# Two layers forward and backward on one core: the first MLP's order of work, a second load of K, and rows turned inside a norm's wait

## The chip, the core and the metric

The kernel runs on one core of a Trainium2 chip. The metric is the device time of one execution in microseconds (us); of the kernel before there are three runs, with a median of 460.42 us (459.21 to 463.47). One more execution was profiled, and every line of a profile comes from that one: it took 461.23 us, with a span of 459.2 us from the first to the last instruction. TensorE's granted clock was 0.629 of full speed on average.

## The reference: what is computed

Two identical decode layers, one token, with weights shared by both, and then the gradients of all inputs for a given `grad_out`:

```python
x = A_x
x = x + attn(layernorm(x)); x = x + mlp(layernorm(x))   # layer 0
x = x + attn(layernorm(x)); x = x + mlp(layernorm(x))   # layer 1
# attn: q = x @ wq (32 heads of 128); the last 4096 of 32768 keys and values, 4 groups of heads
#       p = softmax(q k / sqrt(128)); (p v) @ wo
# mlp:  h = x @ w1 + b1; act = h * tanh(softplus(h)); act @ w2
out, vjp = jax.vjp(f, x, k_cache, v_cache, wq, wo, w1, b1, w2)
return out, *vjp(grad_out)
```

All data are bf16. D = 1024, wq is 1024 x 4096, wo 4096 x 1024, w1 1024 x 3584, w2 3584 x 1024. The gradients of the two caches are as large as the caches (2 x 32 MB); all of them but the last 4096 rows of each group is zero.

## The kernel before: how the work is tiled and staged

The token is one column, so a product with a weight matrix is a row of 128 x 128 weight loads with a moving operand of one column (`mv`, L460; the loops at L493, L573, L621 and L673). A gradient product needs the same matrix turned. For that a row block of a tile is either turned on TensorE (`turned`, L446: eight transposes into a PSUM bank of `big()`, a copy back over the tile by VectorE or ScalarE through `evac`, L297, and eight products some rows later through `later`, L434), or it is multiplied with a broadcast vector and summed on VectorE (`rowdot`, L420). `rows_chunk` (L466) takes the four row blocks of a tile of wo or w2: the first `nr` go to `rowdot`, the others to `turned`. There are three banks `BIG` for all of that; SC[1] is lent as a fourth in the wq stages (L902).

The stages, in order of time: norm, q, scores, softmax, p v, wo of layer 0 (to 70 us); h of the first MLP (to 88); the first MLP's w2 products, with the row blocks of w2 turned for the later gradient in between (L719 to L727), to 105; the attention of layer 1 (to 150.5); its MLP's h (to 161); eight turnings of K and V (`conv(8, "A")`, L767); then backward: w1 of layer 1 (`dn_b1`, 170 to 191), wo of layer 1 (192 to 221), scores (to 232), wq (to 260; its result is the gradient g2 that goes into the next stage), w2 with layer 1's forward products beside it (L1097 to L1102, 262 to 288), w1 of layer 0 (`dn_b0`, to 298), wo (to 321), scores and wq of layer 0 (to 352). From there to 437 the outer products of the weight and cache gradients are made and copied out (the tail), and stores go on to the end.

K and V must stand the other way round in the backward pass than in the forward pass. `conv_units` (L591) lists 32 units of eight blocks, 16 of K and 16 of V; `conv` turns some in place wherever it is called: one after the scores (L514), one in the softmax (L530), one after each wo tile of layer 1 (`wo_hook1`, L740), eight after the MLP (L767), two after each wo tile backward (L955) until none is left. `w1_rest` (L780) does the like for eight units of w1, for use in `dn_b0`: two behind the scores' gradient, two behind dq (`dp3`, `dq3`), four within wq (`dn3`).

What sets the order is the program's own order on each engine and two queues of transfers. SP's queue loads the weights: a `Ring` (L38) of eight slots of 1,024 KB. Loads stand in a fixed list (L272 to L288) and go out when a slot is released; a released slot takes the next one on the list. Five tiles of wq are kept from layer 0 to layer 1 (`KEEP_Q`), so in the first MLP three slots turn round. w2's tile 3 has `zt` as its home (L282). POOL's queue writes the zero part of the cache gradients: 56 blocks of 1,024 KB out of `zt`, which must have been cleared (L728) after tile 3 was used. `zeros(n, after)` (L256) issues n of them; `after` is a value for which POOL waits first.

`ln_bwd` (L391) is the norm's gradient: two small sums on VectorE, one product with `onesD` on TensorE (L406), four small operations on VectorE. Its `beside` is called ahead of and behind that product; only the last stage gives one. The product of a norm and its result leave TensorE waiting.

Of the kernel before, what the change touches and what calls it, by code (L numbers as in the profile page):

```python
# [18 lines left out]
D = 1024  # L19
# [74 lines left out]
def kernel(  # L94
# [296 lines left out]
    def ln_bwd(part, n32, rstd, g, name, beside=None):  # L391

        st = tmp([P, 2], FP32, "bst")
        dn = tmp([P, TD], FP32, "dn")
        t2 = tmp([P, TD], FP32, "t2")
        if part is None:
            nc.vector.tensor_scalar(out=dn[:], in0=TP[:, 0:TD], scalar1=1.0, scalar2=0.0, op0=ALU.mult, op1=ALU.add,
                                    accum_out=st[:, 0:1])
        else:
            nc.vector.scalar_tensor_tensor(out=dn[:], in0=TP[:, 0:TD], scalar=1.0, in1=part[:], op0=ALU.mult, op1=ALU.add,  # L400
                                           accum_out=st[:, 0:1])
        nc.vector.scalar_tensor_tensor(out=t2[:], in0=dn[:], scalar=1.0, in1=n32[:], op0=ALU.mult, op1=ALU.mult,
                                       accum_out=st[:, 1:2])
        if beside is not None:
            beside()
        nc.tensor.matmul(TP[:, 128:130], lhsT=onesD[:], rhs=st[:], start=True, stop=True)  # L406
        if beside is not None:
            beside()
        ab = tmp([P, 2], FP32, "ab")
        nc.vector.tensor_copy(ab[:], TP[:, 128:130])  # L410
        nc.vector.scalar_tensor_tensor(out=t2[:], in0=n32[:], scalar=ab[:, 1:2], in1=dn[:], op0=ALU.mult,
                                       op1=ALU.subtract)
        nc.vector.tensor_scalar(out=t2[:], in0=t2[:], scalar1=ab[:, 0:1], scalar2=rstd[:, 0:1], op0=ALU.add,
                                op1=ALU.mult)
        gn = sb([P, TD], FP32, f"g_{name}")
        nc.vector.tensor_sub(gn[:], g[:], t2[:])
        return gn
# [27 lines left out]

    def turned(w, n, mv, eng=None, block=None):  # L446

        b = big().bitcast(BF16)
        for i in range(n):
            nc.tensor.transpose(b[:, i * P:(i + 1) * P], block(w, i) if block else w[:, i * P:(i + 1) * P], ident_bf[:])  # L450
        evac(w, b[:, 0:n * P], eng, cost=(0.69 * n / 8, n / 8))
        later(mv, True)

# [11 lines left out]

    def rows_chunk(ch, c, col, l, vec, dst, off, nr=2, eng="A"):  # L466

        for tt in range(4):
            r = 4 * c + tt
            if tt < nr:  # L470
                rowdot(ch[:, tt, :], [vec], D, dst[:, r:r + 1])
            else:
                w = ch[:, tt, :]
                turned(w, TD, lambda w=w, r=r: mv(w, TD, TP[:, off + r:off + r + 1], lambda i: col[:, i, l:l + 1], True), eng)

# [5 lines left out]
    def attn_fwd(l, x, st, first, wo_hook, q_hook=None):  # L481
# [4 lines left out]
        if q_hook is not None:  # L486
            q_hook()
        q_ps = MV[:, 0:HQ]
        order = list(range(TD)) if l == 0 else sorted(range(TD), key=lambda t: t not in KEEP_Q)
        for k, t in enumerate(order):  # L490
# [4 lines left out]
            if l == 0 and t in KEEP_Q:  # L495
                ring.keep(("q", 0, t), ("q", 1, t))
            else:
                ring.release(("q", l, t))
        qv = QC[:].rearrange("p v (g u l h) -> p v g u l h", g=G, u=2, l=2)
        nc.vector.tensor_scalar(out=qv[:, 0, :, 0, l, :], in0=q_ps.rearrange("p (g h) -> p g h", g=G), scalar1=scale,  # L500
# [12 lines left out]
        if not first:  # L513
            conv(1, "A")  # L514
        nc.vector.tensor_tensor(out=m64[0][:], in0=m64[0][:], in1=m64[1][:], op=ALU.max)
        m32 = small[:, 128:160]
# [12 lines left out]
        if not first:  # L529
            late = conv_pe(1)  # L530
        for i in range(2):
# [18 lines left out]
        for u in range(2):  # L550
            nc.tensor.matmul(TP[:, 256:288], lhsT=onesD[:], rhs=ssv[:, :, u, :], start=(u == 0), stop=(u == 1))

        rs = small[:, 288:320]
        nc.vector.tensor_scalar(out=rs[:], in0=TP[:, 256:288], scalar1=float(D), scalar2=None, op0=ALU.mult)
# [35 lines left out]

    conv_units = [(KT, g, b8) for g in range(G) for b8 in range(4)] + [(VS, g, b8) for g in range(G) for b8 in range(4)]  # L591
    conv_units.reverse()
# [22 lines left out]
    def mlp_fwd(l, x, st):  # L615
        name = f"B{l}"
        n32, rstd = ln_fwd(x, st, NB[:, :, l], name)
        h_ps = MV[:, 192:192 + TF]
        for t in range(TD):
# [98 lines left out]
    mv_open()  # L718
    for c in range(7):  # L719
        ch = ring.get(("2", 0, c))  # L720
        mlp_out(0, ch, c, y_ps)
        flush()
        if c in EARLY_2:
            ring.release(("2", 0, c))
        elif c < 6:
            rows_chunk(ch, c, GB, 1, gbc, da1, DA)
            later(lambda c=c: ring.release(("2", 0, c)))  # L727
    nc.gpsimd.memset(zt[:], 0.0)  # L728
    x2, st2 = residual(y_ps, x1, "B0")


    def last_da():

        rows_chunk(ring.get(("2", 0, 6)), 6, GB, 1, gbc, da1, DA)
        flush()
        ring.release(("2", 0, 6))
        v = da1[:, 8:TF].rearrange("p (a b) -> p a b", b=4)[:, :, 2:4]
        nc.vector.tensor_copy(v, TP[:, DA + 8:DA + TF].rearrange("p (a b) -> p a b", b=4)[:, :, 2:4])

    def wo_hook1(c):  # L740
        if c == 0:
            zeros(7, OC[:, 0, 1:2])
        conv(1)

# [21 lines left out]
    put_by("NB", NB, TD)  # L766
    conv(8, "A")  # L767
    mp1 = sB1["deriv"]()
# [22 lines left out]
    def dn_b1(g):  # L791
# [10 lines left out]
        flush()  # L802
        return ln_bwd(dnp, sB1["n32"], sB1["rstd"], g, "B1")

# [21 lines left out]
    def dn_b0(g):  # L826
        bcast(lambda c: DHC[:, c, 0:1], STAY)
        mv_open()
        for t in range(TD):
# [8 lines left out]
            if t == 4:  # L838
                rowize_f()
        return ln_bwd(dnp, sB0["n32"], sB0["rstd"], g, "B0")  # L840

    DENSE = 2

    def attn_bwd(l, sv, g, wo_key, wq_key, wq_keep, hooks, beside=None):
# [6 lines left out]
        for c in range(8):  # L851
            ch = ring.get((*wo_key, c))

            behind[0] = max(2, 6 - max(0, c - DENSE + 1))
            rows_chunk(ch, c, GA, l, LB[0], do32, DA, 0 if c < DENSE else 1, None)
            later(lambda c=c: ring.release((*wo_key, c)))
            hooks["do"](c)
# [86 lines left out]
    def dq3():  # L944
        w1_rest(2)
        zeros(4, DQC[:, 0, 1:2])

    def dn3(t):
        if t % 2:
            w1_rest(1)  # L950
        if t in (3, 5):
            zeros(1, dnp[:, t:t + 1])

    g2 = attn_bwd(1, sA1, g3, ("o", 1), ("q", 2), KEEP_Q2,
                  dict(do=lambda c: conv(2), dp=dp3, dq=dq3, dn=dn3))  # L955


# [137 lines left out]
    mv_open()  # L1095
    even()
    for c in range(7):  # L1097
        ch = ring.get(("2", 1, c))
        mlp_out(1, ch, c, y_ps)
        flush()  # L1100
        rows_chunk(ch, c, GB, 0, LB[0], da0, DA)
        later(lambda c=c: ring.release(("2", 1, c)))  # L1102
    flush()
    rows_join(da0, TF, DA)
    nc.vector.tensor_tensor(out=dh0[:], in0=da0[:, 0:TF], in1=mp0[:], op=ALU.mult)
    nc.vector.tensor_copy(DHC[:, :, 0], dh0[:])
# [37 lines left out]
    def dn1(t):  # L1144
        if t in (3, 6, 7):
            zeros(2 if t == 3 else 1, dnp[:, t:t + 1])
        if t == 4:
# [3 lines left out]

    def units_a0():

        even()
        load["D"] += 10
        work(4)
# [51 lines left out]
```

## Time and profile before

| what | value |
|---|---|
| median of three runs | 460.42 us (459.21 to 463.47) |
| profiled execution | 461.23 us, span 459.2 us |
| TensorE products busy | 341.7 us, 74% |
| VectorE, ScalarE, POOL busy | 256.6, 225.0, 38.7 us |
| moved by DMA | 179.38 MB, 391 GB/s on average |
| SP's queue, POOL's queue | 119.74 MB, 58.72 MB |
| zero blocks | 56 of 1,024 KB, first issued at 120.9 us, last at 350.1 us |

A line of a timeline has the start in us, the length, engine, line, operation, what is written and what is read, the count, and in brackets how long the engine was idle before and what released it. A line of the windows has the stretch, its length, the busy time of TensorE (products, then weight loads), VectorE, ScalarE and POOL with the number of instructions, the granted clock, the share of the 16 DMA engines and the rate in GB/s.

### The profile page before, as it was taken

The page shows a single profiled execution, that of the slowest core. Times are in us where ns is not written, and L with a number is a line of the kernel's source. Part 1 is how long each engine was busy: PE and PEld are TensorE (multiplying, and loading weights), DVE is VectorE, ACT ScalarE, POOL GpSimd, SP SyncE. Part 2 cuts the span into 40 slices and gives each one's busy share as a digit, 9 for nine tenths or more (in the row PEclk, how much of TensorE's full clock was granted, in tenths as well). Part 3 has the DMA queues.
Part 4 walks back from the last instruction along what each step waited for, and adds up shares of the span by engine and source line. Part 5 has one row for each costly group of instructions (what it writes and reads, how often), then busy time and mean ns, then how long its engine had stood idle before and what let it go on. Part 6 is the DMA issues. An engine that isn't in the chain of part 4 may idle for free. (4 is left out here: it accounts for less than half of the span.)

```text
span 459.2 us, 14200 instructions
## 1 busy us (share of the span) xinstructions
PE 341.7 (74%) x6361; PEld 276.6 (60%) x6361; DVE 256.6 (56%) x516; ACT 225.0 (49%) x261; POOL 38.7 (8%) x85
## 2 busy tenths in 40 slices
PE   3836445598679888598879798798797888889900
PEld 3735434497569887498779798697693222224600
DVE  4505731283060149677528676657456999998810
ACT  2502001055045379377317555157064999999900
POOL 1000000030103322200211000101221000000000
PEclk9955555555555569699759955589586555555555
DMA  8999999877999999999999988999999999999995
GB/s 337 421 420 418 418 419 416 361 278 261 385 425 422 421 417 418 415 399 415 420 422 418 421 320 298 347 344 368 422 419 424 412 422 422 418 421 416 405 407 213
DMA packets 27802, 179.38 MB, mean 391 GB/s; under 512 B 3642, under 2 KB 3670, under 8 KB 9430
## 3 DMA queue, kind: packets, MB, share of 16 engines
q1 hardware_dynamic: 19586, 119.74, 65.5%
q0 software_dynamic: 8064, 58.72, 30.9%
q8 instruction: 49, 0.80, 0.6%
q14 instruction: 11, 0.09, 0.0%
q10 hardware_dynamic: 92, 0.02, 0.0%
HBM read 79.74 MB, written 98.62 MB: 388 GB/s over the span
## 5 line engine op out<-in xcount | busy, mean ns | idle before, releaser
L306 ACT COPY ring<-BIG 128x1024 bf16<-128x1024 bf16 x62 | 60.7, 1014 | 41.5 <-PE BIG L450 36.1
L450 PE MATMUL BIG<-ident_bf,ring 128*128 128x128 bf16 x744 | 67.4, 255 | 1.8 <-ACT W L306 1.1
L450 PEld LDWEIGHTS <-ring 128*128 128x128 bf16 x816 | 61.5, 116 | 2.8 <-issue 2.2
L1015 PE MATMUL wide<-W 2*128 2x512 bf16 x228 | 52.1, 598 | 9.3 <-ACT W L306 2.0
L427 DVE CUSTOM_DVE_ANT_0 junk<-ring,SC 128x1024 bf16<-128x1024 bf16 x34 | 41.3, 1215 | 5.4 <-DMA ring<-in_B_w_dram 3.7
L1015 PEld LDWEIGHTS <-W 2*128 2x128 bf16 x240 | 12.6, 102 | 44.3 <-issue 43.2
L462 PEld LDWEIGHTS <-ring 128*128 128x128 bf16 x912 | 31.6, 98 | 9.3 <-ACT ring L306 6.7
L306 ACT COPY KT<-BIG 128x1024 bf16<-128x1024 bf16 x22 | 21.8, 1016 | 30.3 <-PE BIG L602 28.7
L303 DVE CAST ring<-wide 128x1024 bf16<-128x1024 f32 (+1 forms) x29 | 33.7, 1199 | 3.2 <-PE wide L1015 1.5
L306 ACT COPY W<-BIG 128x1024 bf16<-128x1024 bf16 x28 | 26.7, 1119 | 16.0 <-PE BIG L788 14.9
L306 ACT CAST ring<-wide 128x1024 bf16<-128x1024 f32 (+1 forms) x35 | 32.9, 1018 | 1.3 <-PE wide L1066 0.5
L303 DVE COPY ring<-BIG 128x1024 bf16<-128x1024 bf16 x31 | 21.3, 690 | 19.3 <-PE BIG L450 12.2
L264 POOL DMA_DIRECT2D out_dram<-zt x56 | 29.7, 534 | 22.9 <-DMA out_dram<-zt 22.0
L621 PE MATMUL MV<-NB,W 128*128 128x1 bf16 x448 | 16.2, 172 | 9.3 <-DMA W<-in_B_w_dram 6.5
L493 PE MATMUL MV<-NA,ring 128*128 128x1 bf16 x512 | 14.9, 165 | 11.0 <-DMA ring<-in_A_wq_dram 8.6
L621 PEld LDWEIGHTS <-W 128*128 128x128 bf16 x448 | 15.9, 118 | 9.8 <-DMA W<-in_B_w_dram 7.2
L303 DVE CAST VS<-wide 128x1024 bf16<-128x1024 f32 (+1 forms) x17 | 19.7, 1186 | 3.6 <-PE wide L1015 3.0
L1066 PE MATMUL wide<-W 32*128 32x256 bf16 x128 | 20.9, 402 | 0.9 <-ACT ring L306 0.8
L306 ACT CAST KT<-wide 128x1024 bf16<-128x1024 f32 x20 | 20.4, 1032 | 1.8 <-PE wide L1015 0.9
L493 PEld LDWEIGHTS <-ring 128*128 128x128 bf16 x512 | 14.2, 103 | 11.5 <-DMA ring<-in_A_wq_dram 9.1
L427 DVE CUSTOM_DVE_ANT_0 junk<-ring,DSX 128x1024 bf16<-128x1024 bf16 x16 | 19.6, 1224 | 1.1 <-DMA ring<-in_B_w_dram 0.7
L427 DVE CUSTOM_DVE_ANT_0 junk<-W,SC 128x512 bf16<-128x512 bf16 (+1 forms) x20 | 15.8, 791 | 6.5 <-PE SC L330 5.8
(268 smaller groups left out, 566.9 us busy)
## 6 DMA issues: line engine op xcount, KB each, us to landing
out_dram<-zt POOLq DMA_DIRECT2D x56, 1024.0 KB, 16.2
ring<-in_A_wq_dram SPq DMA_DIRECT2D x22, 1024.0 KB
ring<-in_A_wo_dram SPq DMA_DIRECT2D x14, 1024.0 KB
ring<-in_B_w_dram SPq DMA_DIRECT2D x13, 1024.0 KB
W<-in_A_wo_dram SPq DMA_DIRECT2D x10, 1024.0 KB
W<-in_B_w_dram SPq DMA_DIRECT2D x8, 896.0 KB
out_dram<-ring SPq DMA_DIRECT2D x7, 1024.0 KB
out_dram<-ring SPq DMA_DIRECT2D x13, 512.0 KB
```

Of the source, the lines that this page charges most:

```text
L264: nc.gpsimd.dma_start(dst, zt[:])
L303: nc.vector.tensor_copy(dst, src)
L306: nc.scalar.copy(dst, src)
L427: nc.vector.tensor_tensor_reduce(out=out, in0=a, in1=vec, scale=1.0, scalar=acc if i else 0.0, op0=ALU.mult, op1=ALU.add, accum_out=acc)
L450: nc.tensor.transpose(b[:, i * P:(i + 1) * P], block(w, i) if block else w[:, i * P:(i + 1) * P], ident_bf[:])
L462: nc.tensor.matmul(out, lhsT=w[:, i * P:(i + 1) * P], rhs=rhs_of(i), start=fresh[0], stop=last and i == n - 1, skip_group_check=True)
L493: nc.tensor.matmul(q_ps[:, h:h + 1], lhsT=ch[:, h * P:(h + 1) * P], rhs=NA[:, t, l:l + 1], start=(k == 0 and h == 0), stop=(k == TD - 1), ...
L621: nc.tensor.matmul(h_ps[:, fb:fb + 1], lhsT=f_block(W1[:, t], fb), rhs=NB[:, t, l:l + 1], start=(t == 0 and fb == 0), stop=(t == TD - 1), ...
L1015: nc.tensor.matmul(b[:, 512 * i:512 * i + 512], lhsT=R[at:at + 2, lo:lo + P], rhs=R[at:at + 2, ro + 512 * i:ro + 512 * i + 512], start=Tru ...
L1066: nc.tensor.matmul(b[:, k * 256:(k + 1) * 256], lhsT=RT[32 * g:32 * g + 32, a, tp, :], rhs=YS[32 * g:32 * g + 32, :], start=True, stop=Tru ...
```

## The change

Five things are done at once.

- First MLP: the w2 products of tiles 0 to 6 go ahead, and the turnings of tiles 2 to 6 are spread between and behind them. Tile 2's row blocks are turned ahead of the first product; tile 5's and tile 6's after the norm, inside layer 1's q (`last_da` with k). Three zero blocks are issued when `zt` is clear.
- K: one group of four is still turned; the other three are loaded again from the cache, as they lie there, once layer 1's scores are done. 20 units are left, and they are called at other places.
- `w1_rest`: two units leave the place behind dq and go into the w2 stage.
- `turn_ahead`: in the norm that precedes w2, and in the one that precedes layer 0's wo, three row blocks of the next stage's first tile are turned into the three `BIG` banks; `rows_chunk` finds them there and only copies them out. In the w2 stage all four row blocks of tile 0 are turned, and SC[1] is lent as a bank.
- Three zero blocks fewer in layer 0's wq stage.

```diff
+    def turn_pe(w, n, block=None):
         b = big().bitcast(BF16)
         for i in range(n):
             nc.tensor.transpose(b[:, i * P:(i + 1) * P], ...)
+        return b
+    def turn_ev(w, b, n, eng=None):
         evac(w, b[:, 0:n * P], eng, cost=(0.69 * n / 8, n / 8))
+    ahead = {}
+    def turn_ahead(key, tts):
+        for tt in tts:
+            ahead[key, tt] = turn_pe(ring.get(key)[:, tt, :], TD)
...
+                if (key, tt) in ahead:
+                    turn_ev(w, ahead.pop((key, tt)), TD, eng)
+                    later(f, True)
+                else:
+                    turned(w, TD, f, eng)
...
         if not first:
             conv(1, "A")
+            for g in range(K_TURNED, G):
+                nc.sync.dma_start(KT[:, g], kv_src(A_k_cache, g))
...
-            late = conv_pe(1)
+            late = conv_pe(2)
...
+    K_TURNED = 1
+    conv_units = [(KT, g, b8) for g in range(K_TURNED) ...] + [(VS, g, b8) for g in range(G) ...]
...
+    da_turn(2)
+    for c in range(3):
+        da_out(c)
         if c in EARLY_2:
             ring.release(("2", 0, c))
+    da_put(2)
+    da_dots(2)
+    da_out(3)
+    da_turn(3)
+    da_put(3)
+    da_dots(3)
+    da_mv(2)
+    da_out(4)
+    da_mv(3)
     nc.gpsimd.memset(zt[:], 0.0)
+    zeros(3)
+    da_turn(4)
+    da_put(4)
+    da_dots(4)
+    da_out(5)
+    da_dots(5)
+    da_mv(4)
+    da_out(6)
     x2, st2 = residual(y_ps, x1, "B0")
...
+    def last_da(k):
+        if k == -1:
+            da_turn(5)
+            da_put(5)
+            da_dots(6)
+        elif k == 1:
+            da_mv(5)
+            da_turn(6)
+            da_put(6)
+        elif k == 3:
+            da_mv(6)
...
     def wo_hook1(c):
-        conv(1)
+        if c in (2, 5):
+            conv(1)
...
-    conv(8, "A")
+    conv(4, "A")
...
         flush()
-        return ln_bwd(dnp, sB1["n32"], sB1["rstd"], g, "B1")
+        conv(3, "A")
+        return ln_bwd(dnp, sB1["n32"], sB1["rstd"], g, "B1", lambda k: conv(k, "A"))
...
-        return ln_bwd(dnp, sB0["n32"], sB0["rstd"], g, "B0")
+        return ln_bwd(dnp, sB0["n32"], sB0["rstd"], g, "B0", lambda k: turn_ahead(("o", 3, 0), ((0,), (1, 2))[k]))
...
     def dq3():
-        w1_rest(2)
         zeros(4, DQC[:, 0, 1:2])
...
-                  dict(do=lambda c: conv(2), dp=dp3, dq=dq3, dn=dn3))
+                  dict(do=lambda c: conv(1 if 1 <= c <= 5 else 0), dp=dp3, dq=dq3, dn=dn3),
+                  lambda k: turn_ahead(("2", 1, 0), ((0,), (1, 2))[k]))
...
+    bigs.append(SC[1])
     for c in range(7):
         mlp_out(1, ch, c, y_ps)
         flush()
-        rows_chunk(ch, c, GB, 0, LB[0], da0, DA)
+        rows_chunk(ch, c, GB, 0, LB[0], da0, DA, 2 if c else 0, "A" if c else None, ("2", 1, c))
+        if c in (2, 4):
+            w1_rest(1)
...
     def dn1(t):
-        if t in (3, 6, 7):
-            zeros(2 if t == 3 else 1, dnp[:, t:t + 1])
+        if t == 3:
+            zeros(1, dnp[:, t:t + 1])
```

In the diff `da_out`, `da_dots`, `da_turn`, `da_put` and `da_mv` are one tile's products, its two row sums on VectorE, its two turnings on TensorE, their copies by ScalarE, and the products with the turned blocks together with the tile's release. Two single units of `conv` stand, besides, behind the softmax's sum and behind the norm of layer 1's MLP.

## The prediction, made before the result was known

> **What bounds the kernel now.** I read the page's slices first, then the windows by stage, then the timelines of SP, POOL and TensorE, last the clock in windows of 3.4 us.
>
> The page, part 2 and the totals (40 slices of 11.48 us):
>
> ```profile
> PEclk9955555555555569699759955589586555555555
> DMA  8999999877999999999999988999999999999995
> GB/s 337 421 420 418 418 419 416 361 278 261 385 425 422 421 417 418 415 399 415 420 422 418 421 320 298 347 344 368 422 419 424 412 422 422 418 421 416 405 407 213
> DMA packets 27802, 179.38 MB, mean 391 GB/s; under 512 B 3642, under 2 KB 3670, under 8 KB 9430
> ```
>
> The transfers stand at 415 to 425 GB/s nearly everywhere; they dip only in slices 7 to 10 and 23 to 27. So the time is bytes over rate, plus what the dips lose. The windows price that (window, length, engines' busy time, clock, DMA share, GB/s):
>
> ```profile
> 8.00:88.00 80.00, 45.18 (x1155) 42.19 (x1153) 27.84 (x62) 12.10 (x16) 0.21 (x1) 0.59 1.01 420
> 88.00:112.00 24.00, 19.11 (x427) 18.44 (x427) 17.01 (x50) 12.91 (x16) 3.51 (x1) 0.50 0.71 260
> 112.00:128.00 16.00, 10.99 (x358) 10.25 (x355) 1.99 (x5) 0.80 (x1) 1.41 (x3) 0.50 0.99 379
> 128.00:264.00 136.00, 114.18 (x2371) 108.33 (x2372) 73.06 (x184) 75.88 (x87) 22.12 (x47) 0.74 1.01 417
> 264.00:320.00 56.00, 49.82 (x1041) 46.96 (x1038) 38.12 (x82) 30.18 (x34) 2.47 (x6) 0.65 0.93 333
> 352.00:437.00 85.00, 74.53 (x395) 26.64 (x393) 75.92 (x70) 80.45 (x92) 0.00 (x0) 0.50 1.01 417
> 437.00:459.20 22.20, 0.00 (x0) 0.00 (x0) 1.25 (x2) 0.33 (x1) 0.00 (x0) 0.50 0.77 307
> ```
>
> After 438.3 no engine computes and DMA still has some 15 us of stores to move: the end belongs to DMA. At 417 GB/s the dips lose 24 x (1 - 260/417) = 9.0 us, 16 x (1 - 379/417) = 1.5 us and 56 x (1 - 333/417) = 11.3 us. The first dip, on POOL and SP:
>
> ```profile
> 99.70 3.51 POOL L728 MEMSET zt<- 128x4096 bf16 x1 [63.65 <-PE TP L462]
> 120.90 1.20 POOL L264 DMA_DIRECT2D out_dram<-zt  x2
> ...
> 91.37 5.35 SPq L71 DMA_DIRECT2D ring<-in_B_w_dram  x3
> 102.92 8.54 SPq L71 DMA_DIRECT2D ring<-in_A_wq_dram  x3
> 111.95 8.78 SPq L71 DMA_DIRECT2D ring<-in_A_wo_dram  x8
> ```
>
> The ring has three free slots, so loads wait for chunks to be used up, and no zero block is issued before 120.9, though its source was clean at 103.2. From 120.9 to 262 the 40 zero blocks fill every gap; from 264 only a few remain, and the second dip opens.
>
> **The sum.** 0 to 88 stays. 88 to 104 stays too (below). The end piece, 437 to 459.2, keeps its 22.2 us and 6.8 MB. Between 104 and 437 the kernel moves 179.38 - 35.9 (8 us at 293, 80 at 420) - 4.2 (88 to 104, two windows of 8 us at 275 and 247) - 6.8 = 132.5 MB in 333 us, 398 GB/s; at 417 it would take 317.7, so 15.3 us are lost.
>
> **K loaded twice.** Three tiles of 1,024 KB, 3.15 MB: at 417 GB/s 7.5 us more. They are issued by SP behind the eight wo loads, waiting for layer 1's last score product (126); SP has nothing else until 152.6, so that wait holds nobody. They land by 165 at worst and are read first at 227.6. In return 12 of 32 turnings go: 8 transposes at 0.10 us (0.83) cold or 0.056 (0.445) warm, and one 1.0 us copy on ScalarE each. On the path: layer 1's wo loop loses six (13.4 us, of which 6 x 0.81 = 4.9); the block of eight after the MLP becomes four (five units take 4.23 us, so 4 x 0.85 = 3.4 off the start of the 18.6 us stage that VectorE bounds; three go behind that stage's turnings, where TensorE waits 3.02 us for VectorE); the wo loop of the backward pass goes from 14 units to 5 (9 x 0.445 = 4.0 us). The extra unit in the softmax hides under the 0.71 us wait for EX or costs up to 0.8; those beside the norms hide in waits of 1.1 to 3.0 us, and cost 0.83 each if these are gone.
>
> **First MLP.** Products first: 7 x 0.9 us. Chunk 2's turning (1.66 us) goes ahead of them, into a wait of 2.41 us for AC; but W1's last tile landed at 86.84 and a tile takes 2.49 (the spacing of the wo products, one tile each), so chunk 2 is there near 89.3 and the products start 0.6 us late, at 91.0. Adding up TensorE's order, chunk 2 is released at 97.0 (96.4 before), so chunk 6 is no earlier; x2 comes near 103.3 instead of 105.45, as one turning (1.66) and its products (0.7) go behind it. VectorE's eight dots keep their order and end at 102.6. Chunk 3 is used at 98.7, the 3.5 us memset ends at 102.3, and three zero blocks go out on POOL, 19 us ahead of today's first: data from 104. They are the three that leave the last wq stage (issued 344 to 350, where DMA is full). Nobody needs POOL between. The two turnings inside q cost 2 x (1.66 + 0.7) against one before, so q gains nothing from x2: near 120 to 122, either side of 120.4, since its last wq tile now shares the engines with zeros.
>
> **Last four w1 units.** Two leave the place after dq: from the broadcast (231.86) to the first turned row (237.42) 5.6 us shrink by 3.1 (the 1.56 us "issue" gap stays) to 4.7. They reappear in the w2 stage: 2 x 0.83 at most. There chunk 0's two dots (2.5 us of VectorE) turn into turnings, too: VectorE and ScalarE share four copies of 0.69 or 1.0.
>
> **Rows turned ahead.** 24 transposes inside each norm's wait. Before w2 (260.1 to 262.2, clock 0.96) 8 + 16 take 0.45 + 0.9 us beside VectorE's chain: nothing added. Before wo (295.7 to 298.3, clock 0.50) 0.83 + 1.66 overrun waits of 0.48 and 1.50 by about 0.5. Each takes 1.3 to 2.5 us off the next stage, if chunk 0 has landed. If it has not, TensorE stands in front of the norm's product and the norm is late with it; chunk 0 was issued 15 us ahead in both. The clock:
>
> ```profile
> 166.40:169.80 3.40, 3.40 (x35) 3.40 (x33) 0.00 (x0) 3.40 (x5) 0.53 (x1) 0.50 1.03 415
> 170.00:173.40 3.40, 3.09 (x54) 2.69 (x51) 2.60 (x7) 3.40 (x5) 0.94 (x2) 1.00 1.02 424
> 262.10:265.50 3.40, 3.28 (x55) 3.28 (x56) 2.23 (x4) 0.50 (x1) 0.63 (x2) 0.50 1.01 424
> ```
>
> A window of transposes alone (166.4 to 169.8) brings full clock; the w2 stage, half transposes, half one-column products, never gets it. Entered warm it would need 2.1 us a chunk on TensorE instead of 3.3 and be bound by VectorE's 2.54. The Trainium skill, "TensorE: Matmul & The Clock Gate", Part 4, says that transposes do not count as TensorE being busy, so turning ahead could not hold the clock; this trace says otherwise. By that rule the w2 stage would keep its 26 us and end 3 us later, under 2 us of it in the time.
>
> **Where the stalls go.** Later loads share DMA with zeros. A tile of w2 issued at 267.43 was waited for until 276.59 with one zero block under way:
>
> ```profile
> 276.59 1.01 PE L673 MATMUL MV<-AC,ring 128*128 128x1 bf16 x32 [0.93 <-DMA ring<-in_B_w_dram]
> ```
>
> With zeros queued all the time I estimate half rate, 5 us a tile. Then layer 1's wo tiles land until about 148 to 151 and eat the 4.9 us of the wo loop (gain -1.5 to 4.9; I take 0); after that the chain gains 3.4 + 4.0 + 3.1 = 10.5 us up to w2. There w2's tiles, at 5 us each, take part back; I take the tail's start at 345 instead of 352 (bounds 338 to 358).
>
> Is DMA full then? Between 104 and g2 (the gradient behind layer 1's attention, 261.9 now) it has six tiles more to move than now, 15 us, of which the filled first dip pays 3.1 + 1.5 = 4.6; so zeros are queued 10 us beyond the point where they now run out (266), and compute stands 10 us earlier. In the 56 us of the second dip DMA moves 18.7 MB now; 20 us more in front are 8.3 MB, and 27.0 MB would need 65 us: full, and I take 1 us for places where the order leaves a gap (bounds 0 and 11.3). The tail does not forbid it: its DMA view has 39.85 MB of stores, 95.6 us at 417; with 6 us behind the last byte, 345 + 101.6 = 447.
>
> Sum: 459.2 - 15.3 + 7.5 + 1.0 = 452.4 us of span. The profiled execution took 461.23, 2.0 over its span, and 0.8 over the median of 460.42: 453.6, say 453.5 for the median.
>
> **The rivals.**
> 1. *The second dip stays.* If loads slow the chain by what the turnings save, the zeros are used up early and the later loads still wait for slots: 459.2 + 7.5 - 4.6 - (0 to 5) = 457 to 462, for the median 458 to 463. For it: ring loads are released by compute, one at a time. Against: the six added tiles alone are 15 us of work. 0.22.
> 2. *Slower: loads at half rate.* Fifteen tiles are loaded between g2 and the tail; at 5 us that is 75 us of the 83 us those stages take now, and K's tiles stand in the same queue before them. If the tail starts after 362, 362 + 101.6 + 1.2 passes 465: the point is ten us of load waits beyond today's. I would put it at 466. The Trainium skill, "DMA: Bandwidth & Descriptors", section "Queues, rings and completion order", says each DMA engine takes the queues in turn by packet, which is this sharing; the 9.2 us above agree. 0.13.
> 3. *The first dip closes further*, or the rate is 421: 3 to 5 us less, 448 to 451. Against: chunk 6 is issued no earlier. 0.15.
>
> **How the numbers follow.** The forecast has 0.50, with its own range 451 to 457. About 1% (4.6 us) is what a measurement here can tell from no change: under 455.8 is faster. The forecast gives 0.44 to that and case 3 0.15: 0.59. Same: 0.06 + 0.21 = 0.27. Slower: 0.13 and 0.01. The range leaves out half of case 2 and the ends of 1 and 3: 448.5 to 463.
>
> **What would show it.** Right: zero blocks from near 102, GB/s near 417 from 104 to the tail, no L602 on KT beyond four units, K's tiles landed before 170, clock 1.00 past g2, compute of the tail ending before 437. Wrong: a dip under 380 GB/s left after g2 (case 1), or long TensorE waits on ring tiles in layer 1's wo and in w2, and a tail starting after 352 (case 2).

## The result, and the profile after

| | before | after |
|---|---|---|
| median (range), 20 runs each | 460.20 us (459.21 to 463.47) | 461.96 us (460.64 to 463.44) |
| ratio, 95% interval | | 1.0037 [1.0026, 1.0049] |
| profiled execution, span | 461.23, 459.2 us | 462.77, 461.0 us |
| moved by DMA | 179.38 MB | 182.53 MB |

The time hardly moved: 0.4% slower, inside the 1% that I called no change, and 8.5 us above the forecast of 453.5. The page of the changed kernel, part 2 (40 slices of 11.53 us) and the total:

```profile
PEclk9955555555555569898689755596677555555555
DMA  8999999878999999999999999999997699999997
GB/s 337 421 419 419 420 418 418 348 274 311 424 422 423 422 421 423 424 406 421 423 424 423 422 424 424 420 341 367 421 421 285 263 412 415 417 415 418 406 408 315
DMA packets 28234, 182.53 MB, mean 396 GB/s; under 512 B 3690, under 2 KB 3718, under 8 KB 9478
```

The wide dip of slices 23 to 27 has become a small one (26 and 27). The first dip, slices 7 to 9, is nearly as it was. And a dip is there that before did not have: slices 30 and 31, counted from 0, at 285 and 263 GB/s, where before has 424 and 412. The windows of the changed kernel (stretch, length, busy time of TensorE's products and weight loads, VectorE, ScalarE, POOL, then clock, DMA share, GB/s) place it:

```profile
88.00:104.00 16.00, 11.89 (x288) 11.73 (x288) 12.52 (x35) 6.43 (x9) 3.05 (x1) 0.50 0.66 256
104.00:112.00 8.00, 6.17 (x141) 5.92 (x139) 4.26 (x15) 4.55 (x6) 2.19 (x4) 0.50 0.86 287
112.00:128.00 16.00, 10.57 (x349) 10.34 (x348) 1.05 (x3) 1.93 (x2) 1.20 (x3) 0.50 1.01 418
128.00:264.00 136.00, 112.31 (x2437) 105.71 (x2434) 75.76 (x190) 73.03 (x83) 21.61 (x46) 0.75 1.01 421
264.00:320.00 56.00, 43.74 (x831) 41.26 (x830) 28.89 (x66) 24.19 (x28) 3.00 (x7) 0.59 0.99 399
...
352.00:362.00 10.00, 6.92 (x68) 2.62 (x65) 6.20 (x18) 6.47 (x12) 0.00 (x0) 0.50 0.24 100
362.00:437.00 75.00, 66.28 (x348) 23.01 (x347) 69.41 (x64) 71.36 (x80) 0.00 (x0) 0.50 1.02 414
```

From 352 to 362 DMA runs at a quarter: the last zero block was issued at 348.00, and there is nothing to store yet. The timeline of SP in the changed kernel, the first store of the tail:

```profile
360.78 0.82 SPq L1068 DMA_DIRECT2D out_dram<-VS  x2
```

and the same in the kernel before:

```profile
355.53 1.90 SPq L994 DMA_DIRECT2D out_dram<-VS  x2
```

The tail starts 5.25 us later (3.4 to 5.25 us, counted against three executions of the code before, see the experiments); the forecast had it 7 us earlier. Priced like the prediction's dips, (1 - rate/417) x length, the idle time of DMA moved instead of going away: 352 to 368 runs at 216 GB/s (7.7 us lost), 264 to 352 at 403 (3.0, before 11.0), 88 to 112 at 266 (8.7, before 9.0). The marks of the stages (start, us) show where the chain lost what it had gained:

| stage | before | after | later by |
|---|---|---|---|
| first MLP's w2 products | 90.35 | 92.06 | 1.7 |
| scores, layer 1 | 120.64 | 124.53 | 3.9 |
| h of layer 1's MLP | 153.66 | 156.98 | 3.3 |
| scores backward, layer 1 | 222.39 | 219.13 | -3.3 |
| g2, the w2 stage | 262.22 | 256.00 | -6.2 |
| `dn_b0` | 288.68 | 285.70 | -3.0 |
| wo backward, layer 0 | 298.27 | 296.49 | -1.8 |
| scores backward, layer 0 | 322.13 | 327.07 | 4.9 |
| first store of the tail | 355.53 | 360.78 | 5.2 |

3 to 4 us are lost by 125, 9.5 us won from 157 to 256, and 11.5 us lost from 256 to 361. The timeline of TensorE in the changed kernel shows the last loss, first in the w2 stage, then at layer 0's wo:

```profile
270.28 1.01 PE L701 MATMUL MV<-AC,ring 128*128 128x1 bf16 x32 [1.08 <-DMA ring<-in_B_w_dram]
...
275.18 1.01 PE L701 MATMUL MV<-AC,ring 128*128 128x1 bf16 x32 [0.88 <-DMA ring<-in_B_w_dram]
...
280.17 1.01 PE L701 MATMUL MV<-AC,ring 128*128 128x1 bf16 x32 [1.82 <-DMA ring<-in_B_w_dram]
...
311.26 1.03 PE L450 MATMUL BIG<-ident_bf,W 128*128 128x128 bf16 x8 [5.44 <-DMA W<-in_A_wo_dram]
```

The last tiles of w2 come 4.9 to 5.0 us apart, and TensorE waits for each; before, the tiles were used 2.6 to 4.5 us apart, with one wait. On SP the loads of wo stand behind small moves of rows, one of which takes 6.08 us to issue (0.50 us before, at 295.02); they go out at 301.67 (297.28 before), and their first tile is used 9.6 us after that:

```profile
291.58 6.08 SPq L832 DMA_DIRECT2D W<-dr_NA  x1
297.75 3.81 SPq L888 DMA_DIRECT2D W<-W  x2
301.67 2.79 SPq L71 DMA_DIRECT2D W<-in_A_wo_dram  x3
```

The first MLP is no better for its loads. The timeline of TensorE, then that of POOL, in the changed kernel:

```profile
90.39 1.89 PE L450 MATMUL BIG<-ident_bf,ring 128*128 128x128 bf16 x16 [2.51 <-DMA ring<-in_B_w_dram]
...
92.06 2.74 PE L701 MATMUL MV<-AC,ring 128*128 128x1 bf16 x96
...
99.40 1.01 PE L701 MATMUL MV<-AC,ring 128*128 128x1 bf16 x32 [1.60 <-DMA ring<-in_B_w_dram]
...
104.94 1.01 PE L701 MATMUL MV<-AC,ring 128*128 128x1 bf16 x32 [0.84 <-DMA ring<-in_B_w_dram]
```

```profile
100.95 3.51 POOL L785 MEMSET zt<- 128x4096 bf16 x1 [65.11 <-PE TP L469]
104.77 1.73 POOL L264 DMA_DIRECT2D out_dram<-zt  x3 [0.31 <-POOL zt L785]
```

Tile 2 is there at 90.39, and the products start at 92.06 (forecast 91.0). The zeros are issued at 104.77, not near 102, and the first dip closes by 0.3 us in 88 to 112 and by 1.5 us to 128.

### The profile page after: what moved, and what is told of

Read it like the earlier page. It is cut to its first block, busy times and chain, and to the rows that moved or that the text cites. A ratio compares the mean times of both kernels' runs of the same rounds, so it can differ in the third digit from the quotient of the medians.

```text
span 461.0 us, 14067 instructions
## 1 busy us (share of the span) xinstructions
PE 336.6 (73%) x6297; PEld 271.4 (59%) x6297; DVE 251.7 (55%) x509; ACT 219.6 (48%) x255; POOL 38.3 (8%) x83
## 2 busy tenths in 40 slices
DMA packets 28234, 182.53 MB, mean 396 GB/s; under 512 B 3690, under 2 KB 3718, under 8 KB 9478
## 3 DMA queue, kind: packets, MB, share of 16 engines
q0 software_dynamic: 8064, 58.72, 30.6%
## 4 chain that ended last, share of the span: by engine, by line
PE 37%; DMA 35%; DVE 9%; ACT 9%; issue 5%; ACTq 0%; SPq 0%; DVEq 0%
PE BIG L450 10%; DMA ring<-in_B_w_dram 8%; DMA ring<-in_A_wq_dram 7%; DMA W<-in_A_wo_dram 7%; DMA ring<-in_A_wo_dram 6%; PE TP L469 5%; DMA W<-in_B_w_dram 4%; ACT ring L306 4%; PE wide L1140 4%; DVE junk L427 3%; PE wide L1089 3%; DMA W<-in_A_k_cache_dram 2%; ACT W L306 2%; PE MV L701 2%; ACT KT L306 2%
## 5 line engine op out<-in xcount | busy, mean ns | idle before, releaser
L306 ACT COPY ring<-BIG 128x1024 bf16<-128x1024 bf16 x58 | 57.3, 1013 | 50.0 <-PE BIG L450 36.3
L450 PE MATMUL BIG<-ident_bf,ring 128*128 128x128 bf16 x728 | 65.4, 252 | 3.1 <-DMA ring<-in_B_w_dram 2.5
L450 PEld LDWEIGHTS <-ring 128*128 128x128 bf16 x832 | 62.1, 115 | 3.7 <-DMA ring<-in_B_w_dram 2.6
L427 DVE CUSTOM_DVE_ANT_0 junk<-ring,SC 128x1024 bf16<-128x1024 bf16 x32 | 38.9, 1215 | 10.0 <-DMA ring<-in_B_w_dram 9.6
L469 PEld LDWEIGHTS <-ring 128*128 128x128 bf16 x928 | 32.6, 99 | 10.0 <-issue 6.0
L264 POOL DMA_DIRECT2D out_dram<-zt x56 | 29.8, 534 | 88.2 <-DMA out_dram<-zt 87.6
L306 ACT COPY W<-BIG 128x1024 bf16<-128x1024 bf16 x27 | 25.8, 1069 | 19.6 <-PE BIG L450 10.9
L303 DVE COPY ring<-BIG 128x1024 bf16<-128x1024 bf16 x33 | 22.5, 690 | 15.0 <-PE BIG L450 13.2
L450 PE MATMUL BIG<-ident_bf,W 128*128 128x128 bf16 x216 | 19.1, 243 | 6.0 <-DMA W<-in_A_wo_dram 6.0
L512 PEld LDWEIGHTS <-ring 128*128 128x128 bf16 x512 | 14.7, 103 | 14.0 <-DMA ring<-in_A_wq_dram 14.0
L1140 PE MATMUL wide<-W 32*128 32x256 bf16 x128 | 20.9, 402 | 0.9 <-ACT ring L306 0.8
L306 ACT CAST KT<-wide 128x1024 bf16<-128x1024 f32 x20 | 20.4, 1032 | 1.8 <-PE wide L1089 0.9
L649 PEld LDWEIGHTS <-W 128*128 128x128 bf16 x448 | 15.8, 118 | 9.0 <-DMA W<-in_B_w_dram 7.2
```

What stands on the lines that cost most here:

```text
L264: nc.gpsimd.dma_start(dst, zt[:])
L303: nc.vector.tensor_copy(dst, src)
L306: nc.scalar.copy(dst, src)
L427: nc.vector.tensor_tensor_reduce(out=out, in0=a, in1=vec, scale=1.0, scalar=acc if i else 0.0, op0=ALU.mult, op1=ALU.add, accum_out=acc)
L469: nc.tensor.matmul(out, lhsT=w[:, i * P:(i + 1) * P], rhs=rhs_of(i), start=fresh[0], stop=last and i == n - 1, skip_group_check=True)
L512: nc.tensor.matmul(q_ps[:, h:h + 1], lhsT=ch[:, h * P:(h + 1) * P], rhs=NA[:, t, l:l + 1], start=(k == 0 and h == 0), stop=(k == TD - 1), ...
```

## The experiments

Two theories were put to the chip. S, mine after the result: the chain is shorter by about the forecast's 10 us, but later loads share DMA with zero blocks at half rate, so the gain goes back and the tail starts late. Against it stood readings in which one part is to blame: K's bytes alone, the three early zero blocks alone, or the slow move on SP. The kernel before gave medians of 459.98, 460.13, 460.45 and 459.71 us beside the four groups of runs, so a difference between runs of two groups is good to about 0.7 us. The ratios are those on record and need not equal those of the medians.

Every mark of a stage comes from one profiled execution, and marks of equal code differ. Up to the tail, the two runs at the end of this section with products behind the tail are the kernel before: g2 stands at 262.22, 260.86 and 263.21, the first store at 355.53, 357.37 and 356.77. The two runs of rows turned ahead have g2 at 261.21 and 256.60, the first store at 354.67 and 354.96. So a mark at g2 is good to about 5 us, and a first store to about 2.

Each part alone comes first.

**K loaded twice, alone.** Before, with the second load and the 20 units at the change's places.

```diff
+            for g in range(K_TURNED, G):
+                nc.sync.dma_start(KT[:, g], kv_src(A_k_cache, g))
...
+    K_TURNED = 1
-    conv(8, "A")
+    conv(4, "A")
```

> The kernel before with one part of the change: three groups of K loaded again, 20 units of turning at the places that the change gives them; first MLP, zeros and rows ahead as before. Theory S (sharing: what is added to DMA early halves the rate of the ring loads and then is missing where the tail starts): the 7.5 us of K fill part of the second dip, since the chain gains some 10 us up to g2 and then waits for loads; 459 to 462, tail's first store within 3 us of 355.5. Rival K (the reload is paid in full and is the whole loss): 465 to 468.

Measured: 462.51 us, ratio 1.0041 [1.0014, 1.0068]. g2 comes at 254.21, 8.0 us before its old time, which fits the 3.4 + 4.0 us forecast for the turnings that go, as far as one mark at g2 can tell. But the first store comes at 355.98, 0.4 us later than before, and DMA is full at 352. The 3.15 MB are paid and the chain's gain is lost between 254 and 356.

**The new order of the first MLP, alone,** with its three early zero blocks (in the old kernel they are issued in layer 0's wq).

> The kernel before with the new order of the first MLP alone, and with its three zero blocks early instead of in the last wq stage. Theory S: q's and wo's tiles of layer 1 share DMA with the three zero blocks, scores start some 3 us later, wo is not longer than before by more than 2; the three blocks are missing at the tail's start: 460 to 464. The forecast's reading (bytes moved out of the full stretch into a dip): 456 to 458.

```diff
+    da_turn(2)
+    for c in range(3):
+        da_out(c)
...
+    zeros(3)
...
-        if t in (3, 6, 7):
+        if t == 3:
```

Measured: 462.43 us, ratio 1.0024 [0.9989, 1.0059]. Scores of layer 1 come at 125.46, 4.8 us late; the first store at 361.12, 5.6 us late. The interval holds 1, so the time itself is not shown to be longer. But this part lengthens the chain instead of filling the first dip (9.3 us lost there, 9.0 before).

**Rows turned ahead, alone,** with the two moved units of w1.

```diff
+        return ln_bwd(..., "B0", lambda k: turn_ahead(("o", 3, 0), ((0,), (1, 2))[k]))
...
-        w1_rest(2)
...
+        rows_chunk(ch, c, GB, 0, LB[0], da0, DA, 2 if c else 0, "A" if c else None, ("2", 1, c))
```

> The kernel before with rows turned ahead, tile 0 of w2 wholly turned and two w1 units moved, nothing else. Bytes are unchanged. Theory S: 3 to 5 us off the chain at g2 and about 2 at wo, DMA goes dry no earlier, so the second dip gets shorter in time: 456 to 459. Rival (w2 waits for its tiles 4 to 6 whatever TensorE does): within 1 us of before, 459.5 to 461.

Measured: 458.88 us, ratio 0.9962 [0.9933, 0.9991], and once more, in the third group:

> The kernel before with rows turned ahead alone, a second time, for a narrower interval. Theory S and the first run: 457.5 to 459.5, faster than before by 0.2 to 0.6%. Rival (the first run's gain was chance): 459.5 to 460.5.

458.70 us, ratio 0.9959 [0.9943, 0.9975]. This is the one part that pays: no byte is added, both intervals lie below 1, and the first store comes at 354.67 and 354.96. It beats both kernels, by little.

Now the changed kernel, with one thing undone at a time.

**The three zero blocks late.**

```diff
     nc.gpsimd.memset(zt[:], 0.0)
-    zeros(3)
...
-        if t == 3:
-            zeros(1, dnp[:, t:t + 1])
+        if t in (3, 6, 7):
+            zeros(2 if t == 3 else 1, dnp[:, t:t + 1])
```

> The changed kernel with its three early zero blocks put back into layer 0's last wq stage. Theory S: layer 1's wq and wo tiles land sooner, the 3.9 us wait in wo goes, the tail starts some 3 to 5 us earlier, and the three blocks fill the idle stretch that the changed kernel has at 353 to 362: 454 to 458. The forecast's reading (the first dip opens again by up to 7.5 us): 464 to 469.

Measured: 462.70 us, ratio 1.0047 [1.0017, 1.0076]. The chain is 3.5 us sooner at the scores (121.03), 5.2 at g2 (250.79) and 6.2 at the first store (354.56): at the scores and the first store, 3 MB of zeros in the first MLP's last waits cost the chain that much (at g2 the difference is no larger than what equal code shows). DMA is full from 112 to the stores, as its windows show:

```profile
88.00:112.00 24.00, 18.12 (x425) 17.71 (x426) 16.66 (x48) 10.98 (x14) 3.51 (x1) 0.50 0.62 228
112.00:264.00 152.00, 125.28 (x2863) 118.09 (x2860) 79.20 (x197) 79.17 (x90) 23.58 (x50) 0.74 1.01 418
264.00:352.00 88.00, 69.32 (x1459) 62.35 (x1459) 47.97 (x110) 35.65 (x45) 9.69 (x23) 0.67 0.99 404
352.00:368.00 16.00, 12.68 (x61) 3.11 (x61) 13.92 (x13) 15.10 (x19) 0.00 (x0) 0.50 1.01 415
...
437.00:453.00 16.00, 0.00 (x0) 0.00 (x0) 0.25 (x1) 0.00 (x0) 0.00 (x0) 0.50 1.01 405
453.00:461.00 8.00, 0.00 (x0) 0.00 (x0) 0.00 (x0) 0.00 (x0) 0.00 (x0) 0.50 0.05 22
```

And yet the time is not shorter: the 454 to 458 that I expected by S was missed. Here the start of the tail no longer decides, the bytes do: the first dip (10.9 us), K's 7.5 us, and a last piece, 453 to 461, in which DMA moves 22 GB/s at a share of 0.05, about one engine of 16. In the changed kernel the same stretch moves 274 GB/s:

```profile
453.00:461.00 8.00, 0.00 (x0) 0.00 (x0) 0.00 (x0) 0.00 (x0) 0.00 (x0) 0.50 0.69 274
```

**The first MLP wholly as before.**

```diff
-    da_turn(2)
...
+    for c in range(7):
         ch = ring.get(("2", 0, c))
+        mlp_out(0, ch, c, y_ps)
...
-    zeros(3)
```

> The changed kernel with the old order of the first MLP and all zero blocks where they were before: K loaded twice and rows turned ahead stay. Theory S: chain as in the run with late zeros (tail's first store near 353 to 355), no idle stretch at the tail, the end set by bytes with K's 7.5 us in them: 459 to 462. Rival (the early zeros and the new order are the whole loss): 455 to 457.

Measured: 462.51 us, ratio 1.0040 [1.0018, 1.0062]; first store at 353.96. The same picture: the tail starts 6.8 us sooner than in the changed kernel, the idle time is 12.8 us (9.2, 0.4, 3.2, 0), and nothing is gained.

**K wholly turned,** units at their old places.

```diff
-    K_TURNED = 1
+    K_TURNED = G
...
-    conv(4, "A")
+    conv(8, "A")
```

> The changed kernel with all of K turned again at the old places: new order of the first MLP with its early zeros and rows turned ahead stay. Theory S: no K bytes, but the chain has its turnings back and the early zeros beside its loads, tail's first store at 358 to 361, idle before it: 460 to 463. If K's bytes were the only loss: 454 to 456.

Measured: 460.94 us, ratio 1.0011 [0.9991, 1.0030], 1.0 us less than the changed kernel, little more than the groups differ by. The bytes are gone, but g2 is back at 262.69, and the tail (358.76) still starts late.

**K's second load left out,** the units as in the change; three of four groups of K then lie the wrong way round in the backward pass, so this leaves out the load and nothing else of the time.

```diff
-            for g in range(K_TURNED, G):
-                nc.sync.dma_start(KT[:, g], kv_src(A_k_cache, g))
```

> The changed kernel without the second load of K (three of four K groups stay turned the wrong way, so that this part of the computation is left out), turnings as in the change. If K's 7.5 us were paid in full: 454 to 455. Theory S: the tiles were paid only where DMA was the bound; without them DMA goes dry sooner before the tail, whose first store comes 2 to 4 us earlier (fewer zeros beside the loads): 457 to 460.

Measured: 455.65 us, ratio 0.9902 [0.9879, 0.9925]; 6.3 us less than the changed kernel, where K's bytes are 7.5 us at 417 GB/s. Both forecasts were missed. The size is near that of the bytes, but it is the tail's start that moves, to 354.73, 6.0 us sooner, and the span ends 100.0 us after it, as in the changed kernel (100.2). The start is won in layer 0's wo stage, 23.8 us instead of 30.6: from 290 to 312 zero blocks take 2.1 MB of DMA there, and 3.2 MB in the changed kernel. SP is hardly quicker in this run; one small move is, but the pair behind it is not:

```profile
291.76 0.55 SPq L830 DMA_DIRECT2D W<-dr_NA  x1
294.97 5.70 SPq L886 DMA_DIRECT2D W<-W  x2
300.78 1.70 SPq L71 DMA_DIRECT2D W<-in_A_wo_dram  x3
```

The loads of wo go out 0.9 us sooner than in the changed kernel, and their first tile is used 6.5 us after that instead of 9.6.

**No zero blocks at all,** in the changed kernel and in the one before; the zero part of the two cache gradients is left out.

```diff
-    zjobs.reverse()
+    zjobs.clear()
```

> The changed kernel with no zero block at all (56 MB of the cache gradients are not written). No load shares DMA with zeros. Theory S: q, wo, w2 and the second wo wait less; against the changed kernel the scores start 3 to 4 us sooner, g2 comes 12 to 18 us sooner (near 238 to 244), w2 takes 21 to 23 us instead of 29.7, and the tail's first store comes near 330 to 338. Rival (the waits are release chains of the ring, not sharing): g2 within 5 us of 256, w2 27 to 30 us.

> The kernel before with no zero block at all (56 MB of the cache gradients are not written), to stand beside the changed kernel without them: 432.7 us, g2's broadcast at 243.4, layer 0's dq broadcast at 309.0. If the change shortens the chain when nothing shares DMA, as the forecast's 10.5 us up to g2 say: g2 at 253 to 257, dq at 322 to 328, time 442 to 450. Rival (the chain is no shorter, the change only moves work): g2 within 4 us of 243.

Measured, one execution each: 432.68 us and 445.68 us. Without zeros g2 comes at 243.43 in the changed kernel and at 253.03 in the old one, 9.6 us apart (the forecast's chain gained 10.5), and the first store at 331.03 and 344.08, 13 us apart. So the change does shorten the chain; it is the sharing that takes it back. With zeros the w2 stage takes 29.7 us in the changed kernel and 25.2 without; layer 0's wo 30.6 and 20.9. In the old kernel these two take 26.5 and 23.9 with zeros, 25.0 and 24.5 without.

**The small moves of rows issued by ScalarE** instead of SP, so that no load stands behind them.

```diff
-        nc.sync.dma_start(ROWS[base:base + 2, ...
+        nc.scalar.dma_start(ROWS[base:base + 2, ...
```

> The changed kernel with the small row moves of the first w1 gradient stage and of the wo and wq stages issued by ScalarE instead of SP. Theory S with two bounds (end = the later of: all bytes at 417 GB/s plus what the dips lose; tail's first store plus about 100 us): SP no longer stands 6 us at such a move, the three wo tiles go out some 4 to 6 us sooner, the 5.4 us wait in wo shrinks to under 2, the tail's first store comes at 355 to 357 instead of 360.8 and its idle stretch closes by as much: 456 to 459. Rival (the wait is one for DMA's bandwidth, not for SP): 461 to 462, the wait of 5 us stays.

Measured: 466.86 us, ratio 1.0144 [1.0121, 1.0167], a miss. The wo tiles are issued 10 us sooner (291.60), but now ScalarE stands, and the copies out of PSUM with it (its timeline, then TensorE's wait for it):

```profile
301.86 7.10 ACTq L888 DMA_DIRECT2D W<-W  x2
...
309.06 1.93 ACT L306 COPY ring<-BIG 128x1024 bf16<-128x1024 bf16 x2 [7.22 <-DMA W<-W]
...
310.12 0.26 PE L1048 MATMUL BIG<-ident_bf,GA 128*16 128x128 bf16 x1 [5.52 <-ACT ring L306]
```

The wait for wo's tiles is gone, but another has come in its place. The stall goes with the moves, whoever issues them. Why such an issue takes 6 to 7 us here is open.

**Four zero blocks moved to the end of layer 0's wq,** to feed DMA until the stores come.

```diff
-    zeros(2, dh0)
...
-            zeros(2, do1_acc[:, 4 * c:4 * c + 1])
...
+        if t in (3, 6, 7):
+            zeros({3: 1, 6: 2, 7: 2}[t], dnp[:, t:t + 1])
```

> The changed kernel with four later zero blocks (two issued behind w2, two in layer 0's wo) moved to the last wq stage. Theory S: less sharing in wo, tail's first store 1 to 3 us earlier, and DMA has 10 us of zeros where it was idle from 353 to 362: 454 to 458. Rival (the idle stretch is only where the time shows, and the zeros leave an equal dip at 285 to 320): 460 to 463.

Measured: 460.73 us, ratio 1.0026 [1.0012, 1.0039], 1.2 us less than the changed kernel. The tail's start is full (410 GB/s) and comes at 354.91. Layer 0's wo stage takes 24.7 us instead of 30.6, and its first tile from SP is used 6.7 us after the issue instead of 9.6: with two zero blocks fewer beside them, the loads come sooner. But 264 to 352 falls to 380 GB/s: 7.8 us lost there instead of 3.0. Of that, 4.2 us are lost in one stretch, in which SP's loads stand behind its small moves until 301.49 and few zero blocks are under way (363 GB/s in the changed kernel):

```profile
296.00:302.00 6.00, 5.88 (x83) 5.41 (x81) 3.67 (x11) 3.12 (x4) 0.00 (x0) 0.71 0.32 124
```

So the idle time moves once more, as the rival to S had it, and the time lies in the rival's 460 to 463.

Set side by side, the profiled executions sort into two kinds (idle in us at 417 GB/s):

| run | 88-112 | 112-264 | 264-352 | 352-368 | sum | first store | span | difference |
|---|---|---|---|---|---|---|---|---|
| after | 8.7 | -1.5 | 3.0 | 7.7 | 17.9 | 360.78 | 461.0 | 100.2 |
| new MLP alone | 9.3 | -0.7 | 10.6 | 6.9 | 26.1 | 361.12 | 461.0 | 99.9 |
| K turned | 8.7 | -0.7 | 8.4 | 7.1 | 23.5 | 358.76 | 459.0 | 100.2 |
| K left out | 8.9 | -1.1 | 8.0 | 3.7 | 19.5 | 354.73 | 454.7 | 100.0 |
| moves by ScalarE | 8.8 | -1.5 | 7.6 | 5.5 | 20.4 | 363.22 | 463.4 | 100.2 |
| no zeros, old and new | | | | | | 344.08, 331.03 | 443.9, 430.9 | 99.8, 99.9 |
| before | 9.0 | 1.5 | 11.0 | 0.0 | 21.5 | 355.53 | 459.2 | 103.7 |
| zeros late | 10.9 | -0.4 | 2.7 | 0.1 | 13.3 | 354.56 | 461.1 | 106.5 |
| old MLP | 9.2 | 0.4 | 3.2 | 0.0 | 12.8 | 353.96 | 460.9 | 106.9 |
| K alone | 9.1 | 0.0 | 4.9 | 0.0 | 14.0 | 355.98 | 460.2 | 104.2 |
| zeros to the tail | 9.2 | -1.5 | 7.8 | 0.3 | 15.8 | 354.91 | 459.0 | 104.1 |
| ahead alone | 9.1 | 2.2 | 8.0 | 0.4 | 19.7 | 354.67 | 457.3 | 102.6 |
| ahead alone, again | 9.2 | 1.1 | 9.9 | 0.3 | 20.5 | 354.96 | 457.0 | 102.0 |

In the upper kind the span ends 99.8 to 100.2 us after the first store, whatever came before it: the tail's start decides. In the lower kind DMA is full at the start of the tail and the bytes decide. The changed kernel needs both to come sooner, and each part that pulls one leaves the other.

**What ends last in the lower kind.** The two kernels with K's load, a full start of the tail and the first MLP's zeros late lose 8.2 and 8.7 us less to idle time than before and pay 7.5 for K; by that they should be some 1 us shorter, and they are 1.7 to 1.9 us longer. What such a sum of means leaves out is the last piece: from 453 to 459 they move 28 and 29 GB/s at a share of 0.07, where before still moves 47 at 0.12. I tried whether code, fetched by DMA, makes that engine late, with one-column products behind the last one of the kernel before, into a bank that nobody reads: 256 of them, and 512.

```diff
     work(10000)
+    for _ in range(256):
+        nc.tensor.matmul(wide[0][:, 0:1], lhsT=ident_bf[:], rhs=ident_bf[:, 0:1], start=True, stop=True)
```

> The kernel before, with 256 one-column products (512 TensorE instructions, 32 KB of code) behind the last product of the tail, into a bank that nobody reads. They need 8 us of TensorE by the 1.01 us that 32 such products take, 438 to 446, and nobody waits for them. Theory L (one engine is late by the code): before has 49 packets of instructions, 0.80 MB, with 0.6% of 16 engines' span, 44 us, so some 0.9 us each; two more on the one engine that ends last add 1.8 us: span 461.0, ratio 1.004, and the piece at a share of 0.06 grows by as much. Rival (one engine is late by uneven stores): 32 KB over 417 GB/s, 0.1 us: ratio 1.000.

> The same with 512 products (1,024 instructions, 64 KB, four packets); TensorE runs on to 454 by the same reckoning. Theory L: 3.6 us, span 462.8, ratio 1.008. Rival: ratio 1.000 while TensorE ends ahead of the stores; if it doesn't, the span ends with TensorE and this run tells nothing.

Measured: 460.81 us, ratio 1.0029 [1.0005, 1.0054], and 462.78 us, ratio 1.0068 [1.0047, 1.0089]. The first is 1.3 us (0.2 to 2.5) longer, which fits the 1.8 us of the code and not quite the 0.1 us of the bytes. But in its profiled execution the stores run on at 410 GB/s to 455, after a tail that starts 1.8 us later than before's, and the last piece is not longer, as the theory wanted. In the second TensorE itself goes on to 460.8, so it tells nothing of that. With the zeros late the share is 0.06 to 0.07 in each microsecond from 454 to 459, which is what one engine of 16 at work would give; no view names the engine, and why it ends last is open.

## Why the prediction was wrong, point by point

**The step that failed** is "I take the tail's start at 345 instead of 352". The start came 5.25 us later than before, 12 us from what I took. It breaks the next step, "Is DMA full then? ... I take 1 us": full it is up to 352, and then it has nothing to move, 7.7 us. In the sum this is the term of 15.3 us to be won, less 1.0: between 104 and 437 DMA moved 402 GB/s (398 before), so 12.0 us of idle time stayed where the sum left 1.0.

How it came about: the prediction had the half rate right ("I estimate half rate, 5 us a tile"; measured 4.9 to 5.0) and the gain of the chain right where nothing shares DMA (10.5 us; 9.6 without zeros, 6.2 with them), and wrote that w2's tiles "take part back". They take all of it back, since the sum stopped at w2. The wo tiles of layer 0 stand in the same queue at the same rate, with slow issues of small moves in front: this stage alone goes from 23.9 to 30.6 us, w2 from 26.5 to 29.7, so 9.9 us are lost in two stages. The Trainium skill, "DMA: Bandwidth & Descriptors", section "Queues, rings and completion order", has each engine serve its queues in turn; the spacing of w2's tiles agrees. I used that rule for a rival and not for the sum.

**The first dip** was mis-sized: 4.6 us refilled in the sum, 1.8 measured (0.3 from 88 to 112, 1.5 from 112 to 128, which now runs at 418 GB/s). Tile 2 came 1.1 us later than reckoned and tile 4 was waited for by 1.60 us, so the zeros came at 104.77; tile 6 was waited for by 0.84 us, and the product of the norm behind x2 started at 106.43 (105.98 before) instead of 2 us sooner. Then the zeros stood beside layer 1's wq and wo tiles. I took that to cost q nothing ("q gains nothing from x2") and the wo loop no more than its own gain; with the blocks late, the scores are 3.5 us sooner and the tail's start 6.2.

**The second dip** closed nearly as forecast: 264 to 320 at 399 GB/s, 2.4 us left of 11.3. Taken by itself this step was right, and it bought nothing: the zero blocks that fill it slow w2's and wo's loads (four of them moved away, the wo stage is 5.9 us shorter), and the tail's start then lacks them.

**K's 7.5 us** were right in size, and partly by luck. K alone pays them as bytes: the idle time is 7.5 us less and nothing is won. In the changed kernel the load costs 6.3 us, but through the tail's start, which it puts 6.0 us later; that is not how the sum has it. Its use on the chain fits the forecast: 8.0 us at g2 for K alone.

**Rows turned ahead** were right in that they cost no byte and shorten the time, alone by 0.4%. What they do to the clock is not settled. With them, the 8 transposes of g2's broadcast take 0.62 us in every execution (1.03 before), at a granted clock of 1.00 in the changed kernel (0.50 before); but they also take 0.62 us in one execution of the code before, the run with 256 products behind the tail. The changed kernel, the kernel before, and that run:

```profile
256.00 0.62 PE L330 MATMUL SC<-ident_bf,GB 128*128 128x128 bf16 x8 [0.34 <-DVE GB L1164]
262.22 1.03 PE L330 MATMUL SC<-ident_bf,GB 128*128 128x128 bf16 x8 [1.25 <-DVE GB L1090]
260.86 0.62 PE L330 MATMUL SC<-ident_bf,GB 128*128 128x128 bf16 x8 [1.26 <-DVE GB L1090]
```

So these rows do not decide on the sentence of the Trainium skill, "TensorE: Matmul & The Clock Gate", Part 4, that the prediction names. Nor did the warm entry last. In the changed kernel the clock fell 3 us into the w2 stage, with TensorE busy, and 10 us before its first wait for a tile:

```profile
258.00:259.00 1.00, 1.00 (x36) 1.00 (x35) 1.00 (x2) 0.59 (x2) 0.00 (x1) 0.95 1.08 451
259.00:260.00 1.00, 1.00 (x37) 1.00 (x35) 0.96 (x3) 0.52 (x1) 0.00 (x0) 0.50 0.95 401
```

Without zeros it fell about 5 us into that stage (0.53 from 248 to 249). So the prediction's 2.1 us a chunk stayed out of reach with and without waits for tiles.

**The rivals.** Rival 2 is what happened in its mechanism, but short of the point from which it would make the kernel slower by over 1%: the tail starts at 357.3 (352 + 5.25), not after 362; 357.3 + 101.6 gives 458.9 of span, 461.0 was measured. I gave it 0.13, as a case apart, though it is a scale with the forecast at its other end. Rival 1's number (458 to 463) held the time, for another reason: the second dip did not stay, it moved to the tail. Rival 3 fell: 88 to 112 still loses 8.7 us.

## What to carry to other kernels

A kernel like this one, whose DMA is full most of the time, has two ends: the bytes with their idle time, and the start of the last stage that makes its own bytes. Reckon both for a change, each with its own sum; a part that pulls one alone moves the idle time to another place. Work that fills a gap in DMA is not free if loads on the chain come behind it: price every later load at the shared rate through to the end, not in the first stage only.

## What was not expected of the hardware

- The issue of a 4 KB move of a row took 6.08 us on SP (6.68 with the zeros late, 0.50 before), while loads and zero blocks were queued. Where it took 0.50 to 0.55 us (K alone, K left out), the pair of 7 KB moves behind it took 5.7 us (1.56 before), and on ScalarE that pair took 7.10.
- TensorE stopped at even distances in its code. In the run with 512 products behind the tail, the products stop after each 128 to 134, 256 to 268 instructions, with "issue" as the only cause (TensorE's timeline of that run):

```profile
438.14 3.74 PE L1178 MATMUL wide<-ident_bf 128*128 128x1 bf16 x134
444.13 3.57 PE L1178 MATMUL wide<-ident_bf 128*128 128x1 bf16 x128 [2.26 <-issue]
451.15 3.58 PE L1178 MATMUL wide<-ident_bf 128*128 128x1 bf16 x128 [3.44 <-issue]
457.35 3.41 PE L1178 MATMUL wide<-ident_bf 128*128 128x1 bf16 x122 [2.62 <-issue]
```

  The Trainium skill, "Runtime: NRT & Kernel Launch", section "Instruction fetch mechanics", has code come in blocks of 256 instructions, and the crossing mostly hidden. The 128 products agree with the block; the 2.3 to 3.4 us do not agree with hidden. That a full DMA makes these stops is not shown: at the first two DMA runs at 402 GB/s, but at the third its stores are ending, at 127 GB/s and less from 455 on. In the changed kernel without zeros, where DMA moves 16 GB/s from 243 to 249, 162 products with their weight loads pass without one. In the changed kernel a stop of 2.82 us with "issue" as its only cause lies on the chain ahead of 210.69, and such stops ahead of products with turned row blocks went from 3.0 to 6.6 us in all.
- POOL stood 87.6 us waiting for zero blocks that were still under way (22.0 before).
- Where the bytes decide, the last 6 us of the span hardly use DMA: with the zeros late it moves 28 GB/s from 453 to 459, at a share of 0.07, about that of one of its 16 engines.
